# A fused chunk attention and multiplicative MLP kernel: another written order of steps, and pairs 6 and 7 on the path that joins partitions by DMA

## The chip, the cores and the metric

The kernel runs on one core of a Trainium2 chip. The core has five engines with a queue of instructions each: PE (matrix products, with a lane PEld for loading weights), DVE (vector work), ACT (scalar work and copies), POOL and SP. In this kernel POOL and SP do little but issue DMA transfers. Each engine works through its queue in order; semaphores make one engine wait for another. The metric is device time in microseconds (us), the median of several runs.

## The reference

Attention in chunks of 64 rows, without a mask and within each chunk alone, then a multiplicative MLP on the joined heads:

```
scores = scale * q_c @ k_c^T          # 8 batches, 8 heads, 9 chunks of 64 rows, head width 64
attn   = softmax(scores)              # over the 64 keys of the chunk
x      = (attn @ v_c), heads side by side   # 4608 tokens x 512
a, b   = x @ w1, x @ w2               # 512 -> 1024
out    = ((a * b) @ w3) @ w_out       # 1024 -> 1024 -> 512
```

All inputs and the output are float32. The kernel computes in bfloat16 with float32 sums, multiplies w3 by w_out once (the product w3o, 1024 x 512), and leaves out the maximum of the softmax, with a second path for inputs where that would not do.

## The kernel before

The 4608 tokens are cut into 18 pairs (p = 0 to 17) of 256 tokens, four chunks each, and two pairs make a group g. The whole program is one written list, ORDER, of short names that is walked once; every step issues its instructions at once, and each engine keeps the order of the list. So the list alone sets what stands behind what on PE, DVE, ACT, POOL and SP. A step name is a letter with its numbers:

- POOL issues the loads, with a cast to bfloat16: q, k, v of a pair (256 KB, 256 KB and two of 128 KB; some are cut in two), i (quarters of w1 and w2), o (w_out), h (w3). At most eight loads are under way: each waits for the one eight places ahead of it. q of pair p + 5 also waits until the transposes of pair p have left its buffer, v until the P step that last read its buffer. The steps x11 and x12 make POOL wait for N11.1 and N12.1.
- DVE: T p.s transposes q (s = 0) or k (s = 1) in 32 x 32 blocks (line 201). N p.u divides by the softmax sum (lines 261 and 264), X p.u transposes the result for the MLP (line 297 or 305), M p.j multiplies a and b (line 366), V transposes w3 (line 407).
- PE, all by the helper on line 95: S p are the scores, P p the product with v, A p.j and B p.j the products with w1 and w2 for one slice j, O p the output product for a pair, W the product of w3 and w_out, D fills the time at the start with zeros.
- ACT: E p is the exponential (line 234), C p.j copies a out of PSUM (line 351), Y p copies the output of a pair out of PSUM (line 396), Z copies w3o (line 420).
- SP issues Q p, the store of a pair, and G and H, moves between partitions inside the core (line 193).

Pairs 0 to 3 run A and B for one pair at a time (four slices of two times 256 columns), the later ones for a group (eight slices of 512 columns, named by the group's even pair: A4.0 to A4.7 belong to pairs 4 and 5).

There are two forms of the attention. The first leaves the head's 64 columns split over blocks of 32 partitions: S needs 64 small products that add up in twos, P 64. The second, for pairs 8 to 17, joins halves by DMA: G g.a (two steps of four moves, `qkT` to `qkm`, 128 KB each) ahead of S, which then takes 32 products of 64 x 64, as does P; X then writes `xm`, and H g.a (two steps of four moves, 64 KB each) brings it to `xt` ahead of A and B. The bound is `p < 8` in the code.

The buffers that couple the engines: four PSUM tiles of two banks for all of S, P (two tiles), A with B, O and W, given out in list order as they come free; three copies of a (`a_sb`); two of `e`; two of `qkT`, `qkm`, `xm` and `o_sb`; three of `xn` and `ab`; four of `xt`; five of `qk`; six of v, where pair p takes number p % 6. The first half of an A/B tile holds a, the second b; M reads the copy of a and, from PSUM, b.

In the old list each A p.j is followed on PE by B p.j, and C p.j stands behind both:

```
A4.2 E7 T10.0 B4.2 C4.2 T10.1 P7 v13
```

The functions that the diff touches, and what calls them:

Of the kernel before, what the change touches and what calls it, by code (L numbers as in the profile page):

```python
# [8 lines left out]
ORDER = """  # L9
R0 R1 v0 q1 k1 i0 v1 i1 i2 q2 k2 v2 i3 q3 k3 v3 q4 k4 v4 o h0 h1 D0.0.0.16.64 K0 T0.0 K1 T0.1 q5 k5  # L10
v5 S0 T1.0 E0 P0 D0.1.0.4.512 T1.1 q6 k6 v6 N0.0 S1 D1.0.0.5.512 X0.0 N0.1 X0.1 A0.0 E1 B0.0 C0.0 P1
M0.0 A0.1 N1.0 X1.0 B0.1 C0.1 N1.1 A0.2 X1.1 B0.2 C0.2 M0.1 A1.0 T2.0 B1.0 C1.0 M0.2 A1.1 T2.1 q7 k7
v7 B1.1 C1.1 M1.0 S2 M1.1 A0.3 E2 T3.0 B0.3 C0.3 P2 M0.3 A1.2 N2.0 X2.0 B1.2 C1.2 N2.1 A1.3 X2.1
B1.3 C1.3 M1.2 A2.0 T3.1 q8 k8 v8 B2.0 C2.0 M1.3 S3 T4.0 A2.1 E3 M2.0 B2.1 T4.1 q9 k9 C2.1 P3 v9
M2.1 A2.2 N3.0 B2.2 C2.2 X3.0 A2.3 N3.1 B2.3 X3.1 C2.3 M2.2 S4 M2.3 A3.0 E4 B3.0 C3.0 A3.1 M3.0 B3.1
C3.1 V0 A3.2 M3.1 B3.2 C3.2 V1 A3.3 M3.2 B3.3 C3.3 V2 W0 M3.3 V3 W1 Z0 V4 V5 W2 Z1 V6 V7 T5.0 Z2 W3
T5.1 q10 k10 T6.0 T6.1 P4 v10 q11 k11 Z3 S5 N4.0 O0 E5 X4.0 N4.1 X4.1 T7.0 O1 T7.1 Y0 Q0 T8.0 P5 v11
q12 k12 Y1 S6 T8.1 O2 Q1 E6 N5.0 X5.0 N5.1 X5.1 O3 T9.0 T9.1 Y2 G4.0 P6 v12 q13 k13 A4.0 N6.0 B4.0
G4.1 Y3 X6.0 N6.1 C4.0 A4.1 X6.1 B4.1 C4.1 M4.0 Q2 S7 Q3 M4.1 A4.2 E7 T10.0 B4.2 C4.2 T10.1 P7 v13
q14 k14 A4.3 M4.2 B4.3 N7.0 C4.3 A4.4 X7.0 M4.3 B4.4 C4.4 N7.1 A4.5 M4.4 B4.5 C4.5 X7.1 S8 M4.5 S9  # L20
E8 A4.6 T11.0 B4.6 E9 T11.1 P8 v14 q15 k15 C4.6 A4.7 M4.6 G5.0 B4.7 C4.7 N8.0 A6.0 M4.7 B6.0 N8.1
C6.0 G5.1 A6.1 X8.0 B6.1 M6.0 C6.1 X8.1 P9 v15 A6.2 M6.1 N9.0 B6.2 C6.2 N9.1 A6.3 M6.2 B6.3 C6.3
X9.0 A6.4 M6.3 B6.4 C6.4 X9.1 A6.5 T12.0 H4.0 B6.5 C6.5 M6.4 A6.6 M6.5 B6.6 T12.1 H4.1 C6.6 S10 S11
M6.6 E10 A6.7 T13.0 B6.7 E11 P10 T13.1 C6.7 O4 M6.7 G6.0 N10.0 N10.1 X10.0 G6.1 P11 Y4 X10.1 O5
N11.0 N11.1 x11 q16 k16 v16 Q4 X11.0 X11.1 T14.0 A8.0 H5.0 Y5 B8.0 T14.1 C8.0 A8.1 M8.0 B8.1 H5.1
C8.1 T15.0 A8.2 B8.2 M8.1 C8.2 T15.1 Q5 A8.3 B8.3 C8.3 M8.2 G7.0 S12 M8.3 S13 E12 A8.4 T16.0 B8.4
E13 G7.1 P12 T16.1 C8.4 A8.5 B8.5 M8.4 C8.5 N12.0 A8.6 M8.5 B8.6 C8.6 N12.1 x12 q17 k17 v17 A8.7
M8.6 B8.7 C8.7 X12.0 P13 M8.7 A10.0 X12.1 B10.0 C10.0 N13.0 A10.1 M10.0 B10.1 N13.1 C10.1 A10.2
X13.0 B10.2 M10.1 C10.2 X13.1 S14 S15 M10.2 E14 A10.3 H6.0 T17.0 B10.3 E15 P14 T17.1 C10.3 A10.4
H6.1 M10.3 B10.4 C10.4 N14.0 A10.5 M10.4 B10.5 G8.0 C10.5 N14.1 A10.6 M10.5 B10.6 C10.6 X14.0 P15  # L30
G8.1 X14.1 A10.7 M10.6 B10.7 N15.0 C10.7 O6 N15.1 M10.7 X15.0 X15.1 H7.0 S16 Y6 S17 O7 E16 E17 H7.1
P16 Y7 O8 Q6 N16.0 Q7 N16.1 X16.0 X16.1 P17 Y8 A12.0 N17.0 Q8 B12.0 N17.1 C12.0 A12.1 X17.0 B12.1
M12.0 C12.1 X17.1 A12.2 M12.1 H8.0 B12.2 C12.2 A12.3 M12.2 B12.3 C12.3 H8.1 A12.4 M12.3 B12.4 C12.4
A12.5 M12.4 B12.5 C12.5 A12.6 M12.5 B12.6 C12.6 A12.7 M12.6 B12.7 C12.7 O9 M12.7 O10 Y9 Q9 A14.0 Y10
B14.0 C14.0 Q10 A14.1 M14.0 B14.1 C14.1 A14.2 M14.1 B14.2 C14.2 A14.3 M14.2 B14.3 C14.3 A14.4 M14.3
B14.4 C14.4 A14.5 M14.4 B14.5 C14.5 A14.6 M14.5 B14.6 C14.6 A14.7 M14.6 B14.7 C14.7 O11 M14.7 O12
Y11 Q11 A16.0 Y12 B16.0 C16.0 Q12 A16.1 M16.0 B16.1 C16.1 A16.2 M16.1 B16.2 C16.2 A16.3 M16.2 B16.3
C16.3 A16.4 M16.3 B16.4 C16.4 A16.5 M16.4 B16.5 C16.5 A16.6 M16.5 B16.6 C16.6 A16.7 M16.6 B16.7
C16.7 O13 M16.7 O14 Y13 Q13 O15 Y14 Q14 O16 Y15 Q15 Y16 Q16 O17
"""  # L40


LOW, HIGH = 2.0 ** -60, 2.0 ** 60


@with_exitstack
def first_path(
# [12 lines left out]
    B, H, S, D = q.shape  # L60
# [3 lines left out]
    CH = 64  # L64
# [11 lines left out]
    W = D + 1  # L76
# [215 lines left out]

    def do_X(p, u):
        g, m = divmod(p, 2)
        if p < 8:
            t0 = m * PT + u * UT
            inorder(nc.vector.transpose(  # L297
                new_xt(g)[:].rearrange("p (o t) -> p o t", o=KO)[:, :, t0:t0 + UT]
                .rearrange("p o (m y) -> p m o y", y=BL),
                xn_t[p][:, u].rearrange("p r (c n) (z o) -> p (r c) o n z", c=2, o=KO)))  # L300
# [52 lines left out]
    def do_M(p, j):  # L353
        g = p // 2
        if g not in ab_t:
            ab_t[g] = msb.tile([P, FO, GT], bf, tag="ab", bufs=3, name="ab")
        if p < 4:
            o = ab_t[g][:, 2 * j:2 * j + 2, p % 2 * PT:(p % 2 + 1) * PT]
            view = lambda t: t.rearrange("p (j t) -> p j t", j=2)
        elif p < 8:  # L360
            o = ab_t[g][:, j]
            view = lambda t: t
        else:
            o = ab_t[g][:, j].rearrange("p (c s y) -> p s c y", s=2, y=BL)
            view = lambda t: t.rearrange("p (s c y) -> p s c y", s=2, y=BL)
        inorder(nc.vector.tensor_mul(o, view(a_t.pop((p, j))[:]), view(ps_t.pop((p, j))[:, 1, :])))  # L366
# [201 lines left out]
```

## Time and profile before

| | us |
|---|---|
| median of 3 runs | 244.77 (244.47 to 246.03) |
| span of the profiled execution | 242.9 |
| PE busy | 226.7 (93%) |
| DVE busy | 154.3 (64%) |
| ACT busy | 85.2 (35%) |
| POOL busy, issuing loads | 83.7 (34%) |
| granted clock of PE, mean | 1.00 |

The span runs from the first to the last instruction of one profiled execution, the page gives no other time of that execution; the median of the timed runs is 1.9 us above it. Busy time of PE is counted to modelled ends of pipelined matmuls, so the rows of a group may overlap a little. Digits in the page's slices are tenths, one digit for 6.1 us. A row of the timeline reads: start, length, engine and line, operation, output <- input, shape, count, and in brackets the idle time of that engine just ahead of it with what ended it. A row of the chain: start, length, what. A row of the waits: who waited, for whom, us in all, times, longest.

### The profile page before, as it was taken

How to read it: one execution, taken by the hardware profiler on the slowest of the kernel's cores; microseconds unless marked ns; L12 is line 12 of the kernel's file. 1: busy time of each engine (PE TensorE's matmuls, PEld its weight loads, DVE VectorE, ACT ScalarE, POOL GpSimd, SP SyncE). 2: the span in 40 equal slices, each digit the busy share in tenths (PEclk: the TensorE clock that was granted, in tenths of full speed). 3: DMA queues.
4: the chain of work that ended last, by engine and by line, in shares of the span. 5: the costliest groups of instructions: out<-in, count | busy, mean ns of one | idle time of the engine just before them, and what ended most of it. 6: DMA issues, size and time to landing. Idle time of an engine off the chain costs nothing.

```text
span 242.9 us, 6385 instructions
## 1 busy us (share of the span) xinstructions
PE 226.7 (93%) x2753; PEld 120.2 (49%) x2753; DVE 154.3 (64%) x235; ACT 85.2 (35%) x116; POOL 83.7 (34%) x114
## 2 busy tenths in 40 slices
PE   1189989999999999999999999999999999999994
PEld 1147868874445444444444444444444444444443
DVE  1756799699799588999998899918540332143000
ACT  2412423423333344425336234162332332322322
POOL 7856976656986345764160230000000000000000
PEclk9999999999999999999999999999999999999999
DMA  6999999999999999999999793735502200400244
GB/s 173 179 185 181 185 169 200 196 193 171 167 173 218 222 228 259 179 224 196 205 236 223 221 139 91 163 88 209 142 0 89 87 0 0 173 3 1 86 173 173
DMA packets 93597, 37.65 MB, mean 155 GB/s; under 512 B 75008, under 2 KB 86528, under 8 KB 93568
## 3 DMA queue, kind: packets, MB, share of 16 engines
q0 software_dynamic: 82592, 18.88, 83.9%
q1 hardware_dynamic: 9936, 17.83, 24.0%
q10 hardware_dynamic: 1040, 0.52, 0.8%
q8 instruction: 21, 0.34, 0.6%
q14 instruction: 8, 0.07, 0.1%
HBM read 38.80 MB, written 9.44 MB: 199 GB/s over the span
## 4 chain that ended last, share of the span: by engine, by line
PE 72%; DMA 16%; DVE 4%; SPq 3%; POOL 2%; issue 1%; ACT 0%; DVEq 0%; POOLq 0%
PE ab_ps L95 39%; PE o_ps L95 23%; PE w_ps L95 6%; DMA w<-in_moe_w_dram 4%; DMA qkm<-qkT 3%; SPq L193 3%; DMA qk<-in_q_dram 3%; DMA qk<-in_k_dram 3%; DMA xt<-xm 3%; PE pv L95 2%; PE s_ps L95 2%; DVE qkT L201 2%; POOL vbuf L98 1%; POOL w L98 1%; DVE xt L297 1%
## 5 line engine op out<-in xcount | busy, mean ns | idle before, releaser
L95 PE MATMUL ab_ps<-xt,w 128*128 128x512 bf16 (+1 forms) x688 | 127.4, 342 | 0.7 <-DVE xt L297 0.6
L95 PEld LDWEIGHTS <-w 128*128 128x128 bf16 x704 | 67.1, 98 | 56.1 <-issue 1.8
L366 DVE TENSOR_TENSOR ab<-a_sb,ab_ps 128x512 bf16<-128x512 f32 x71 | 47.8, 674 | 43.4 <-ACT a_sb L351 43.1
L351 ACT COPY a_sb<-ab_ps 128x512 f32<-128x512 f32 x71 | 41.6, 586 | 81.3 <-PE ab_ps L95 81.0
L95 PE MATMUL o_ps<-w3o,ab 128*128 128x512 bf16 (+1 forms) x296 | 63.9, 373 | 0.0
L201 DVE STREAM_TRANSPOSE qkT<-qk 128x1024 bf16<-128x1024 bf16 x36 | 45.1, 1291 | 7.2 <-ACT qk L144 5.5
L95 PEld LDWEIGHTS <-ab 128*128 128x128 bf16 x296 | 28.5, 98 | 32.2
L98 POOL DMA_DIRECT2D vbuf<-in_v_dram x40 | 33.9, 855 | 20.4 <-DMA qk<-in_q_dram 5.2
L396 ACT COPY o_sb<-o_ps 128x1024 f32<-128x1024 f32 x17 | 17.2, 1012 | 45.3 <-PE o_ps L95 41.3
L264 DVE TENSOR_TENSOR xn<-pv,rcs 128x512 bf16<-128x512 f32 x36 | 24.9, 692 | 1.4
L98 POOL DMA_DIRECT2D qk<-in_q_dram x23 | 18.1, 790 | 8.9 <-DMA qk<-in_k_dram 2.4
L98 POOL DMA_DIRECT2D qk<-in_k_dram x23 | 18.0, 783 | 6.5 <-DMA vbuf<-in_v_dram 3.7
L234 ACT ACTIVATE e<-s_ps 128x1024 bf16<-128x1024 f32 x16 | 15.9, 1026 | 1.7 <-PE s_ps L95 1.3
L95 PE MATMUL w_ps<-wo,w3T 128*128 128x512 bf16 x64 | 14.0, 379 | 0.0
L305 DVE STREAM_TRANSPOSE xm<-xn 128x512 bf16<-128x512 bf16 x20 | 13.5, 696 | 0.2
L261 DVE RECIPROCAL rcs<-pv 128x8 f32<-128x8 f32 x36 | 6.9, 193 | 10.4 <-PE pv L95 10.4
L98 POOL DMA_DIRECT2D w<-in_moe_w_dram x16 | 11.1, 695 | 5.3 <-DMA wo<-in_moe_w_out_dram 2.9
L95 PEld LDWEIGHTS <-e 64*32 64x32 bf16 (+1 forms) x832 | 7.8, 97 | 8.7 <-issue 6.9
L95 PE MATMUL pv<-vbuf,e 64*32 64x65 bf16 (+1 forms) x832 | 10.2, 197 | 1.8 <-ACT e L234 1.1
L297 DVE STREAM_TRANSPOSE xt<-xn 128x512 bf16<-128x512 bf16 x16 | 11.4, 711 | 0.5
L389 DVE COPY o_sb<-o_ps 128x256 f32<-128x256 f32 x1 | 0.4, 425 | 16.0 <-PE o_ps L95 16.0
L95 PEld LDWEIGHTS <-qkT 32*64 32x64 bf16 x512 | 5.5, 117 | 10.1 <-DVE qkT L201 7.9
(29 smaller groups left out, 54.2 us busy)
## 6 DMA issues: line engine op xcount, KB each, us to landing
out_dram<-o_sb SPq DMA_DIRECT2D x17, 512.0 KB, 3.3
qkm<-qkT SPq DMA_DIRECT2D x40, 128.0 KB, 4.0
vbuf<-in_v_dram POOLq DMA_DIRECT2D x32, 128.0 KB, 8.2
w<-in_moe_w_dram POOLq DMA_DIRECT2D x16, 256.0 KB, 9.9
qk<-in_q_dram POOLq DMA_DIRECT2D x11, 256.0 KB, 6.8
qk<-in_k_dram POOLq DMA_DIRECT2D x11, 256.0 KB, 7.8
xt<-xm SPq DMA_DIRECT2D x40, 64.0 KB, 3.2
wo<-in_moe_w_out_dram POOLq DMA_DIRECT2D x4, 256.0 KB, 7.1
```

The source lines that it names most:

```text
L95: return inorder(nc.tensor.matmul(*a, **kw))
L98: return inorder(nc.gpsimd.dma_start(dst, src))
L193: inorder(nc.sync.dma_start(dst, src))
L201: inorder(nc.vector.transpose(qkT_t[g][:, :, p % 2, s, heads(h)].rearrange("p e h (y t) -> p h t e y", t=2), qk_t[p][:, s, heads(h)].rearr ...
L234: inorder(nc.scalar.activation(e_t[p][:, :, heads(hh)], s_t[p][:].rearrange("p u (h q) -> p u h q", q=CH)[:, :, heads(hh)], Exp, scale=sca ...
L261: inorder(nc.vector.reciprocal(rc, pv[:, :, :, D:W]))
L264: inorder(nc.vector.tensor_mul(xn_t[p][:, u], pv[:, :, :, 0:D], rc.to_broadcast([P, 2, 4, D])))
L297: inorder(nc.vector.transpose(new_xt(g)[:].rearrange("p (o t) -> p o t", o=KO)[:, :, t0:t0 + UT] .rearrange("p o (m y) -> p m o y", y=BL), ...
L305: inorder(nc.vector.transpose(xm_t[g][:, u, :, m].rearrange("p o (c y) -> p c o y", y=BL), xn_t[p][:].rearrange("p u r m d -> p (u r) m d" ...
L351: inorder(nc.scalar.copy(a_t[p, j][:], ps_t[p, j][:, 0, :]))
L366: inorder(nc.vector.tensor_mul(o, view(a_t.pop((p, j))[:]), view(ps_t.pop((p, j))[:, 1, :])))
L396: inorder(nc.scalar.copy(o_sb[:], ps_t.pop(p)[:]))
```

## The change

Three things. First, the bound `p < 8` becomes `p < MOVED` with MOVED = 6, so pairs 6 and 7 (group 3) take the joined form: the list has the new steps G3.0, G3.1, H3.0 and H3.1. Second, the list is another one from behind B0.2 on; A and B of several slices are interleaved, and a C may stand ahead of its B; pairs come in another order in places (P9 ahead of P8, S13 ahead of S12, O1 ahead of O0, O2 behind O7). Third, v buffers are given out in the order in which P steps free them. Of the old list the diff below shows the first and last changed lines; the new one is whole.

```
--- before.py
+++ after.py
@@ -9,37 +9,38 @@
 ORDER = """
 R0 R1 v0 q1 k1 i0 v1 i1 i2 q2 k2 v2 i3 q3 k3 v3 q4 k4 v4 o h0 h1 D0.0.0.16.64 K0 T0.0 K1 T0.1 q5 k5
 v5 S0 T1.0 E0 P0 D0.1.0.4.512 T1.1 q6 k6 v6 N0.0 S1 D1.0.0.5.512 X0.0 N0.1 X0.1 A0.0 E1 B0.0 C0.0 P1
-M0.0 A0.1 N1.0 X1.0 B0.1 C0.1 N1.1 A0.2 X1.1 B0.2 C0.2 M0.1 A1.0 T2.0 B1.0 C1.0 M0.2 A1.1 T2.1 q7 k7
-v7 B1.1 C1.1 M1.0 S2 M1.1 A0.3 E2 T3.0 B0.3 C0.3 P2 M0.3 A1.2 N2.0 X2.0 B1.2 C1.2 N2.1 A1.3 X2.1
-B1.3 C1.3 M1.2 A2.0 T3.1 q8 k8 v8 B2.0 C2.0 M1.3 S3 T4.0 A2.1 E3 M2.0 B2.1 T4.1 q9 k9 C2.1 P3 v9
-M2.1 A2.2 N3.0 B2.2 C2.2 X3.0 A2.3 N3.1 B2.3 X3.1 C2.3 M2.2 S4 M2.3 A3.0 E4 B3.0 C3.0 A3.1 M3.0 B3.1
...
-C16.3 A16.4 M16.3 B16.4 C16.4 A16.5 M16.4 B16.5 C16.5 A16.6 M16.5 B16.6 C16.6 A16.7 M16.6 B16.7
-C16.7 O13 M16.7 O14 Y13 Q13 O15 Y14 Q14 O16 Y15 Q15 Y16 Q16 O17
+M0.0 A0.1 N1.0 X1.0 B0.1 C0.1 N1.1 A0.2 X1.1 B0.2 A1.2 A1.0 M0.1 C0.2 T2.0 T2.1 B1.2 M0.2 S2 C1.2 q7
+E2 M1.2 P2 B1.0 N2.0 k7 N2.1 A1.3 B1.3 X2.0 C1.0 X2.1 M1.0 T3.0 A2.0 C1.3 A2.3 T3.1 C2.0 A2.2 q9
+B2.0 B2.2 C2.2 M1.3 M2.0 S3 A2.1 T4.0 B2.3 T4.1 q8 B2.1 E3 C2.3 M2.2 P3 C2.1 M2.3 M2.1 S4 N3.0 E4
+N3.1 A1.1 A0.3 X3.0 P4 B0.3 X3.1 C0.3 B1.1 N4.0 M0.3 C1.1 N4.1 A3.0 A3.2 k8 A3.1 M1.1 X4.0 V3 C3.2
+B3.2 A3.3 B3.1 V2 M3.2 C3.1 v9 C3.3 B3.3 k9 V0 M3.1 W1 V1 M3.3 V4 W0 V5 Z0 T5.1 V6 T5.0 V7 X4.1 W2
+T6.0 T6.1 q10 T7.1 Z1 C3.0 S5 W3 E5 B3.0 Z2 Z3 v7 P5 T7.0 N5.0 N5.1 X5.1 O1 X5.0 A4.0 Y1 T8.0 T8.1
+q11 G3.0 B4.0 k11 O0 M3.0 G3.1 A4.7 T9.0 C4.0 Y0 M4.0 T9.1 B4.7 C4.7 S6 S7 M4.7 T10.0 E6 E7 A4.6
+C4.6 q12 P6 B4.6 N6.0 N6.1 M4.6 A4.2 X6.0 C4.2 A4.5 P7 B4.2 G4.0 N7.0 B4.5 A4.1 X6.1 C4.5 v8 N7.1
+A4.3 B4.3 k10 X7.0 G4.1 M4.5 M4.2 C4.3 v10 Q1 B4.1 C4.1 S8 X7.1 S9 M4.3 M4.1 E8 q14 H3.0 E9 O3 T11.1
+Y3 T11.0 P9 N9.0 N9.1 H3.1 q15 T10.1 A4.4 B4.4 C4.4 P8 A6.0 q13 C6.0 N8.0 M4.4 B6.0 A6.7 N8.1 G5.0
+M6.0 k12 A6.1 T12.0 A6.4 A6.2 X8.0 C6.1 B6.2 B6.7 C6.7 B6.1 C6.2 G5.1 B6.4 Q0 M6.7 O4 X9.0 v11 M6.1
+S10 C6.4 M6.4 k13 T14.0 X8.1 M6.2 X9.1 T12.1 E10 H4.0 A6.3 A6.6 Q3 C6.3 k15 Y4 B6.6 T13.0 C6.6 O5
+T13.1 B6.3 M6.6 A6.5 Y5 M6.3 P10 N10.0 C6.5 S11 B6.5 E11 k14 H4.1 A8.0 M6.5 P11 N10.1 C8.0 N11.0 v12
+B8.0 M8.0 T15.1 X10.0 N11.1 G6.0 A8.1 C8.1 T14.1 G6.1 Q4 A8.4 T15.0 O7 O2 X10.1 B8.1 Y7 Q5 S13 B8.4
+X11.0 C8.4 Y2 v13 X11.1 A8.2 E13 M8.1 M8.4 P13 S12 N13.0 B8.2 E12 C8.2 N13.1 H5.0 Q7 M8.2 q16 A8.7
+H5.1 k16 P12 N12.0 N12.1 B8.7 X12.0 O6 G7.0 A10.0 q17 B10.0 G7.1 C8.7 X13.1 T16.0 k17 Y6 X13.0 C10.0
+A10.2 T17.1 x11 A10.4 Q2 C10.4 M10.0 C10.2 T17.0 B10.2 T16.1 B10.4 A8.6 M8.7 M10.4 H6.0 C8.6 G8.0
+B8.6 M8.6 A8.3 S14 v14 S15 M10.2 C8.3 A8.5 E14 C8.5 B8.3 X12.1 A10.1 B8.5 G8.1 B10.1 M8.3 v16 C10.1
+M8.5 v17 E15 M10.1 H6.1 A10.7 C10.7 P14 N14.0 N14.1 X14.0 S16 B10.7 A10.3 E16 v15 A12.0 B10.3 Q6
+C10.3 C12.0 M10.3 O9 M10.7 B12.0 Y9 A12.4 C12.4 M12.0 P15 N15.0 S17 N15.1 B12.4 X15.0 X15.1 E17 O8
+P16 M12.4 X14.1 Y8 H7.0 N16.0 N16.1 A12.5 H7.1 P17 N17.0 B12.5 A12.2 N17.1 B12.2 C12.2 A14.7 A14.0
+C12.5 M12.5 A10.5 B14.0 C14.0 X16.0 C10.5 X17.0 B10.5 M12.2 Q9 M14.0 A12.3 M10.5 A12.6 B12.6 C12.6
+C14.7 M12.6 H8.0 A12.7 X17.1 B14.7 Q8 B12.3 A14.5 M14.7 C12.3 M12.3 A14.6 B12.7 C14.5 C12.7 A12.1
+C14.6 M12.7 B14.5 B14.6 A14.2 B12.1 M14.5 C12.1 A10.6 M14.6 A14.3 X16.1 B14.2 B14.3 M12.1 C14.2
+M14.2 B10.6 O13 C10.6 C14.3 M14.3 H8.1 Y13 A14.4 C14.4 M10.6 A14.1 A16.0 O12 B14.4 Y12 M14.4 B16.0
+C16.0 A16.5 C14.1 A16.1 B16.1 B16.5 M16.0 C16.1 B14.1 C16.5 M14.1 M16.1 A16.6 B16.6 A16.3 B16.3
+A16.4 C16.3 M16.5 B16.4 C16.4 Q13 C16.6 A16.7 M16.3 M16.6 A16.2 C16.7 O15 B16.2 x12 C16.2 Y15 B16.7
+Q15 O10 M16.7 Q12 O14 Y10 Q10 O11 Y14 Y11 M16.2 M16.4 Q14 O16 Y16 Q11 Q16 O17
 """
 
 
+MOVED = 6
 LOW, HIGH = 2.0 ** -60, 2.0 ** 60
 
 
@@ -162,10 +163,13 @@
 
         inorder(nc.gpsimd.tensor_copy(tick[:], xn_t[p][0:1, 1, 0, 0, 0:1]))
 
+    vb_t, vb_free = {}, list(vbuf)
+
     def load_v(p):
+        vb_t[p] = vb_free.pop(0)
         for u in range(2):
             for at, b, c, m in spans(4 * p + 2 * u, 2):
-                load(vbuf[p % 6][at * CH:(at + m) * CH, u, :, 0:D],
+                load(vb_t[p][at * CH:(at + m) * CH, u, :, 0:D],
                      v[b, :, c * CH:(c + m) * CH, :].rearrange("h p d -> p h d"))
 
     def load_w(dst, ap, n0, n1):
@@ -216,7 +220,7 @@
         if p not in s_t:
             s_t[p] = psum("s_ps")
         for h in range(H)[heads(hh)]:
-            if p < 8:
+            if p < MOVED:
                 for e in range(2):
                     for i in range(NB):
                         mm(s_t[p][half[i % 2], i // 2, h * CH:(h + 1) * CH],
@@ -239,21 +243,22 @@
 
 
         e = e_t[p]
+        vb_free.append(vb_t[p])
         for u in range(2):
             if (p, u) not in pv_t:
                 pv_t[p, u] = psum("pv")
             pv = pv_t[p, u]
             for m in range(4):
-                if p < 8:
+                if p < MOVED:
                     for g in range(NB) if hh is None else (2 * hh, 2 * hh + 1):
                         for r in range(2):
                             mm(pv[blk[g], r, m * W:(m + 1) * W],
                                lhsT=e[half[r], u, 2 * g + m % 2, m // 2 * BL:(m // 2 + 1) * BL],
-                               rhs=vbuf[p % 6][half[r], u, 2 * g + m % 2, 0:W], start=True, stop=True)
+                               rhs=vb_t[p][half[r], u, 2 * g + m % 2, 0:W], start=True, stop=True)
                 else:
                     for g, r in ((0, 0), (1, 1), (1, 0), (0, 1)):
                         mm(pv[half[g], r, m * W:(m + 1) * W], lhsT=e[half[r], u, 4 * g + m, :],
-                           rhs=vbuf[p % 6][half[r], u, 4 * g + m, 0:W], start=True, stop=True)
+                           rhs=vb_t[p][half[r], u, 4 * g + m, 0:W], start=True, stop=True)
 
     def do_N(p, u):
         pv = pv_t.pop((p, u))[:, :, 0:4 * W].rearrange("p r (m w) -> p r m w", w=W)
@@ -292,7 +297,7 @@
 
     def do_X(p, u):
         g, m = divmod(p, 2)
-        if p < 8:
+        if p < MOVED:
             t0 = m * PT + u * UT
             inorder(nc.vector.transpose(
                 new_xt(g)[:].rearrange("p (o t) -> p o t", o=KO)[:, :, t0:t0 + UT]
@@ -325,7 +330,7 @@
 
     def do_AB(p, j, f, which):
 
-        if p >= 8:
+        if p >= MOVED:
             rhs = new_xt(p // 2)[:].rearrange("p (s o t) -> p o s t", s=2, o=KO)
         else:
             rhs = new_xt(p // 2)[:].rearrange("p (o t) -> p o t", o=KO)
@@ -357,7 +362,7 @@
         if p < 4:
             o = ab_t[g][:, 2 * j:2 * j + 2, p % 2 * PT:(p % 2 + 1) * PT]
             view = lambda t: t.rearrange("p (j t) -> p j t", j=2)
-        elif p < 8:
+        elif p < MOVED:
             o = ab_t[g][:, j]
             view = lambda t: t
         else:
```

More of the change, by code (lines that the diff above doesn't have):

```diff
@@ L16 @@
[L16 to L37, printed above, removed]
```

## The prediction

> **What bounds the kernel now.** I read the page's busy shares first, then the waits, then the chain that ended last, then the timeline of TensorE.
>
> ```profile
> PE 226.7 (93%) x2753; PEld 120.2 (49%) x2753; DVE 154.3 (64%) x235; ACT 85.2 (35%) x116; POOL 83.7 (34%) x114
> PE   1189989999999999999999999999999999999994
> DVE  1756799699799588999998899918540332143000
> ```
>
> TensorE (PE) is busy 226.7 of 242.9 us, and from the fifth slice on its digit is 9. What it still waits for is in the list of waits of PE:
>
> ```profile
> PE z_ps L95 <- DVE qkT L201: 7.4, 1, 7.4
> PE pv L95 <- ACT e L234: 1.1, 1, 1.1
> PE ab_ps L95 <- DVE xt L297: 0.6, 2, 0.3
> ```
>
> The 7.4 us end at 9.8 us, in the part of the order that stays. Behind that, apart from two gaps of 0.3 us ahead of A1.0 and A2.0 and some short ones with no releaser (0.7 us in P2, 0.5 us in S7), PE waits for nothing. The windows say the same: from 31.8 to 168 us it is busy 135.3 of 136.2 us. So this kernel is bound by the sum of PE's work, and a new order can lower its time only by what PE has less to do; every wait that the order puts on PE is paid in full. Why there are none: in the old list every A is followed by its own B, then the copy C, and between a score step S and its P stand other matmuls. One place has nothing there, S0 E0 P0, and shows the bare price:
>
> ```profile
> 12.02 0.75 PE L95 MATMUL pv<-vbuf,e 64*32 64x65 bf16 x64 [1.13 <-ACT e L234]
> ```
>
> That is one exponential (1.03 us at 10.94) and 0.1 us of hand-over, all seen by PE.
>
> **What the change saves.** The prices of the attention steps are in the chain:
>
> ```profile
> 65.93 0.63 PE pv L95 x64
> 66.56 0.64 PE s_ps L95 x64
> ...
> 95.77 0.64 PE s_ps L95 x64
> 96.41 1.83 PE ab_ps L95 x8
> 98.25 0.38 PE pv L95 x32
> ```
>
> An unjoined P is 64 matmuls in 0.63 us, an unjoined S 64 in 0.64 us. At 95.77 the 64 matmuls are S8 and S9 together, so a joined S takes 0.32 us; a joined P takes 0.38 us. Pairs 6 and 7 save 2 x (0.32 + 0.25) = 1.1 us of PE. The 0.3 us ahead of A2.0 go too, since more matmuls stand there: 1.4 us in all. The transposes X keep their cost (696 ns joined, 711 ns not). The joined path adds 8 qkm and 8 xt moves on SP's queue, 5.0 to 6.0 us of issue per eight. That queue idles 135.8 us waiting for output copies; G3 stands ahead of G4 and 10 us of PE work ahead of S6. I cost the issue at nothing; uncovered it would be 6 us each.
>
> **What the change adds.** In the new list, 27 B steps stand behind their own C (none before), and in the built program the first matmul of such a B then waits for that copy: they share a PSUM tile. The trace of before has no such wait. Bounds: nothing, if the copy is done when PE gets there, and 1.13 us, the nearest row, if all is bare; I take the copy's own row, 0.59 us plus the 0.02 to 0.05 us between engines that the chain shows, and subtract the PE work between. A half step (A or B) is 5.29/6 = 0.88 us, E 1.03 us, Y 1.01 us, M 0.6 us in a row, a transpose T 1.21 us in a row. Walking the new list, the places where the cover is too short:
>
> 1. B1.2 S2 P2: nothing between S2 and P2 on PE, so E2 is bare, 1.1 us as at P0. Before it, M0.1 and two T's (3.0 us after X1.1) against three half steps (2.8): 0.2. Together **1.3**.
> 2. B3.1 B3.3: ACT's list is C3.1, C3.3, and C3.1 waits for B3.1. Two copies bare: **1.25**.
> 3. S6 S7 A4.6 P6 B4.6: ACT does E6, E7 (1.95), then C4.6 (0.6); with hand-over 2.65, less A4.6 and P6 (1.25): **1.4**.
> 4. A6.0 C6.0 B6.0 and A8.6 C8.6 B8.6, with nothing between: 0.65 each, **1.3**.
> 5. B8.4 A8.2 P13: ACT does C8.4, Y2, E13 (0.6 + 1.0 + 1.0 + 0.1), less A8.2 (0.88): **1.8**.
> 6. A10.2 A10.4 B10.2: ACT does C10.4 first, then C10.2: **1.25**.
> 7. Small ones: P14 behind C10.1 and M10.1 (0.45), B8.0 (0.25), B10.7 (0.2): **0.9**.
> 8. A14.7 needs H7.1, which needs X14.1. Behind P15 DVE does two N, two X, M12.4, X14.1 (4.3 us), then SP issues four moves (0.75 each) and the last lands 3.2 us after its issue: some 9.9 us; PE has 8.95 us of work from P15 to A14.7: **1.0**. H3.1 to A6.0 in the same way: **0.2**.
>
> Sum 10.4 us; less 1.4: **+9.0 us**. None is given back later: PE has no wait behind them that could shrink, and the last 60 us of the new list are covered (between C and B lie two steps or more, and O15, O10, O14, O11, O16, O17 follow at 3.46 us each against 1.01 us for the copy and 3.3 us for a store).
>
> Loads: v7 now stands behind q10, which waits for T5.0 (some 62 us); issued by 67 us and landing 8.2 us later (the row of vbuf), P7 at some 86 us has 11 us to spare. q13 waits for T11.0 (some 95 us) with k12, v11, k13 queued behind it on POOL; the first needed of them, k12, is asked for by T12.1 some 17 us later. DVE's own queue waits behind T12.1 and PE behind DVE, so this cover matters; without it the lateness is paid in full. The v buffers given out as they come free change only which P a load waits for. I cost all of this at nothing.
>
> Against its own execution the span becomes 242.9 + 9.0 = 251.9 us. The median of the runs, 244.77 us, lies 1.9 us above that span; with the same around it: **253.8 us**. A difference under 1% (2.4 us) is about what cannot be told from no change.
>
> **The rivals.**
>
> *The waits are half hidden* (chance 0.17). For: my walk counts from modelled ends, and DVE is at 90% from 67 to 130 us (56.5 of 63), so a PE held back lets DVE and the moves catch up; items 1 (0.2), 7 and 8 may vanish (2.1), and each bare copy may show half. Against: the P0 row. Price: about 4.5 us instead of 9, 249.3 us.
>
> *Late transfers* (chance 0.15). A move of qkm lands 4.0 us after its issue in the median but up to 9.2 us; xt 3.2 and up to 8.2. G3 before S6, H3 before A6.0 and H7 before A14.7 have no slack by my walk. Each that lands at its worst costs 5 us: one gives 258.8 us, two 263.8. For: loads keep the DMA at 9 tenths until 110 us. Against: in before all of these were hidden. [...]
>
> *Not slower* (chance 0.08). Mechanism: the single C step. If ACT, busy only 35%, reads each half tile so early that the copy ends within the PE work already queued, no B waits, and S2 to P2 falls where PE would have waited for v2 or w1 loads anyway. Then only the 1.4 us saved remain, and perhaps the 0.02 us by which a half step in the crowded stage (0.88) exceeds one in the last stage (13.81/16 = 0.863), some 1 us over 56 of them: 242.3 us. It decides once six of my nine items show under 0.2 us. That the joining does nothing for pairs 6 and 7 would only add 1.1 us to any case.
>
> **How the numbers follow.** Forecast, waits of 7 to 12 us net: 0.60. The range 248.5 to 260 holds the forecast, most of the half-hidden case and one late move; it leaves out two late moves and the not-slower case. Faster by over 1%: 0.05, within 1%: 0.05, slower: 0.90.
>
> **What would show it.** PE's list of waits should hold some 4 us for ACT e and about 5 us for ACT a_sb, a kind that is absent now, with P2 and P13 the longest single ones; PE's busy time should fall by about 1 us; POOL and the loads should show no new wait of PE. It is wrong if PE waits for DVE or for moves more than for ACT, if the a_sb waits are missing, or if the last chain runs through loads.

## The result, and the profile after

| | before | after |
|---|---|---|
| median of the runs, us | 244.87 (244.47 to 246.03, 4 runs) | 263.38 (262.88 to 264.36, 4 runs) |
| span of the profiled execution, us | 242.9 | 261.9 |

The ratio is 1.077, with a 95% interval from 1.073 to 1.081: slower by 18.5 us between the medians. The forecast was slower by 9.0 us, and its range ended at 260. The direction was right; half of the loss was not foreseen.

The page of the changed kernel: the busy shares, the slices of PE and DVE, the granted clock of PE, and the row of the instruction queue q8.

```profile
PE 230.1 (88%) x2625; PEld 120.8 (46%) x2625; DVE 154.0 (59%) x235; ACT 83.3 (32%) x116; POOL 83.9 (32%) x114
...
PE   1389597779999899899899797999989999998994
...
DVE  1839669697979688838785686456754530332000
...
PEclk9999989999999999999999999999999999999999
...
q8 instruction: 20, 0.33, 0.5%
```

PE has 128 products fewer and is busy 3.4 us longer. That is no contradiction: the busy time is counted to modelled ends, so a matmul in front of a stop counts with its whole length (0.19 us for the product of S4 ahead of its stop, where 64 in a row take 0.71 us), and one at a low clock with more (0.42 us for a product of 128x256 instead of 0.27). The row of slices shows the loss better: at 6.5 us a digit, a 5 and three 7s between 26 and 59 us, two more 7s between 144 and 164, and 8s strewn over the rest. One digit of the clock, behind the 5, is 8 instead of 9. The instruction queue q8 brings 20 packets instead of 21; that row will matter. A move of `qkm` lands 6.7 us after its issue in the median, against 4.0 before.

PE's list of waits in the changed kernel (who waited, for whom, us in all, times, longest):

```profile
PE ab_ps L96 <- ACT a_sb L356: 6.3, 8, 1.2
PE pv L96 <- ACT e L238: 3.9, 3, 1.7
PE s_ps L96 <- issue: 1.9, 1, 1.9
PE pv L96 <- issue: 1.6, 1, 1.6
...
PE ab_ps L96 <- issue: 1.1, 1, 1.1
PE ab_ps L96 <- DVE rcs L266: 1.0, 1, 1.0
PE o_ps L96 <- ACT o_sb L401: 0.7, 1, 0.7
PE ab_ps L96 <- DVE both L286: 0.6, 1, 0.6
```

The first two rows are the forecast: 6.3 us for copies of a (about 5 foretold, a kind that was absent; 1.5 us of the 6.3 stand ahead of B10.5 and B14.7, which were not foretold), and 3.9 us for exponentials (some 4 foretold, one of them P0's as before). The rest was not foreseen. "issue" means that PE waited for nothing that the profile shows.

To place every loss I took, from the timeline of PE, the time from each step's first matmul to the next step's, and subtracted the usual price of the step (a half step 0.92 us in the first pairs and 0.864 later, and the prices of the prediction for S, P and O). What is over comes to 7.4 us before and 27.7 us after. The difference, 20.3 us, less 1.1 us of saved matmuls and 0.2 us of earlier start, is the 19.0 us by which the span grew:

| where | forecast, us | found, us |
|---|---|---|
| the eight numbered places of the prediction | 10.4 | 10.5 |
| copies ahead of B10.5 and B14.7, counted as covered | 0 | 1.8 |
| gaps of PE for "issue" in P2, S4, A3.0, less those of before in P2 and S7 | 0 | 3.7 |
| B1.0, A1.3, B1.3 at a lower clock | 0 | 1.5 |
| DVE or a move late: A8.0 1.1, S6 0.6, S10 0.4, S16 0.4 and less; E for A6.6 0.3 | 0 | 3.1 |
| the last 60 us: O10 0.9, O15 0.3 | 0 | 1.2 |
| start, small waits of before that are gone, and the remainder | -0.3 | -1.7 |
| joined steps of pairs 6 and 7 | -1.1 | -1.1 |
| sum | 9.0 | 19.0 |

Three of the unforeseen losses stand in one stretch of PE's timeline of the changed kernel:

```profile
27.02 0.71 PE L96 MATMUL s_ps<-qkT 32*64 32x64 bf16 x64 [0.17 <-DVE qkT L205]
28.87 0.66 PE L96 MATMUL pv<-vbuf,e 64*32 64x65 bf16 x61 [1.14 <-ACT e L238]
31.12 0.21 PE L96 MATMUL pv<-vbuf,e 64*32 64x65 bf16 x3 [1.59 <-issue]
31.26 5.01 PE L96 MATMUL ab_ps<-xt,w 128*128 128x256 bf16 x29
...
44.01 0.50 PE L96 MATMUL s_ps<-qkT 32*64 32x64 bf16 x37
46.45 0.41 PE L96 MATMUL s_ps<-qkT 32*64 32x64 bf16 x27 [1.95 <-issue]
```

The exponential between S2 and P2 is bare, as foretold. But P2 stops again before its last three products, for 1.6 us, and S4 stops in its middle for 2 us, at no boundary of the written list. And the 29 products behind P2 take 5.01 us, where 0.115 us each would be 3.3.

### The profile page after: what moved, and what is told of

Same layout as the page of the kernel before. It is cut to its first block, busy times and chain, and to the rows that moved or that the text cites. A ratio compares the mean times of both kernels' runs of the same rounds, so it can differ in the third digit from the quotient of the medians.

```text
span 261.9 us, 6172 instructions
## 1 busy us (share of the span) xinstructions
PE 230.1 (88%) x2625; PEld 120.8 (46%) x2625; DVE 154.0 (59%) x235; ACT 83.3 (32%) x116; POOL 83.9 (32%) x114
## 4 chain that ended last, share of the span: by engine, by line
PE 71%; DVE 9%; ACT 6%; issue 6%; DMA 5%; SPq 2%; DVEq 0%; ACTq 0%
PE ab_ps L96 41%; PE o_ps L96 21%; DVE qkT L205 4%; ACT a_sb L356 3%; DMA qkm<-qkT 3%; PE s_ps L96 3%; PE z_ps L96 3%; PE pv L96 2%; DMA raw<-in_q_dram 2%; ACT e L238 2%; DVE xn L269 2%; SPq L197 2%; PE w_ps L96 1%; DVE ab L371 1%; DVE w3T L412 1%
## 5 line engine op out<-in xcount | busy, mean ns | idle before, releaser
L96 PE MATMUL ab_ps<-xt,w 128*128 128x512 bf16 (+1 forms) x688 | 131.5, 345 | 9.7 <-ACT a_sb L356 6.3
L96 PEld LDWEIGHTS <-w 128*128 128x128 bf16 x704 | 68.0, 99 | 67.2 <-issue 11.3
L356 ACT COPY a_sb<-ab_ps 128x512 f32<-128x512 f32 x71 | 40.5, 588 | 95.8 <-PE ab_ps L96 95.7
L310 DVE STREAM_TRANSPOSE xm<-xn 128x512 bf16<-128x512 bf16 x24 | 16.1, 687 | 0.1
L99 POOL DMA_DIRECT2D w<-in_moe_w_dram x16 | 11.1, 696 | 4.5 <-DMA vbuf<-in_v_dram 1.4
L412 DVE STREAM_TRANSPOSE w3T<-w 128x1024 bf16<-128x1024 bf16 x8 | 9.7, 1219 | 1.4 <-PE w_ps L96 1.4
```

Of the source, the lines that this page charges most:

```text
L96: return inorder(nc.tensor.matmul(*a, **kw))
L99: return inorder(nc.gpsimd.dma_start(dst, src))
L310: inorder(nc.vector.transpose(xm_t[g][:, u, :, m].rearrange("p o (c y) -> p c o y", y=BL), xn_t[p][:].rearrange("p u r m d -> p (u r) m d" ...
L356: inorder(nc.scalar.copy(a_t[p, j][:], ps_t[p, j][:, 0, :]))
L412: inorder(nc.vector.transpose(w3T_t[f][:].rearrange("p k (f y) -> p f k y", y=BL), w3[:, NB * f:NB * (f + 1), :].rearrange("p f (k x) -> p ...
```

## The experiments

Where a run has one execution, its span is compared with the 261.9 us of the changed kernel, called the new list here. Four executions of that had spans from 261.3 to 262.8 us, so a difference under 1.5 us in the whole span says little, and the steps are read instead. Of each diff only the steps that move are shown.

**1. All copies behind their B.**

```
-A4.6 C4.6 q12 P6 B4.6
+A4.6 q12 P6 B4.6 C4.6
...
```

All 27 such C move in this manner.

> The changed kernel (span 261.9 us) with one thing undone: each of the 27 copies C that stand ahead of their own B is moved to right behind it. Theory 1, the waits of B for C are paid in full: the eight gaps in which PE waited for a copy of a (B3.3 1.28, B4.6 1.09, B6.0 0.83, B8.0 0.37, B10.2 1.32, B8.6 0.84, B10.5 1.32, B14.7 0.46; 7.5 us) are gone, span 254 to 255.5 us. Rival: they stand for lateness that shows elsewhere once they are gone (DVE, moves between partitions, buffers); span above 258.5 us, with new waits of PE for DVE.

Span 258.6 us, time 260.15 us. The eight waits for `a_sb` are gone from PE's list, and only 3.3 us with them. Two rows of this run's list show what took their place:

```profile
PE s_ps L96 <- DVE ab L371: 1.4, 1, 1.4
PE pv L96 <- DMA qk<-in_q_dram: 1.3, 1, 1.3
```

S13 now waits 1.4 us behind B8.1 for a PSUM tile that DVE has to free. P5 waits 1.3 us in its middle; the row names a load, but ACT's copy Z2, which stands behind C3.0 now, ends at 75.08 us, and PE goes on at 75.13. S10 loses 1.1 us instead of 0.4, part of it to a late `qkm` move. The rival was nearer: the waits taken from PE were in part handed on, to DVE, to ACT's queue and to a move. Of the 7.5 us that the theory expected, 4.2 were given back.

**2. A half step between S2 and P2, and 3. four idle products there.**

```
-S2 C1.2 q7 E2 M1.2 P2 B1.0
+S2 C1.2 q7 E2 M1.2 B1.0 P2
```

```
-S2 C1.2 q7 E2 M1.2 P2 B1.0
+S2 C1.2 q7 E2 M1.2 D2.2.0.4.512 P2 B1.0
```

> The changed kernel with B1.0 moved to stand between S2 and P2. Theory 2, three costs hang on that place: the wait for E2 falls from 1.14 to about 0.2 us, the gap inside P2 (1.79 us behind matmul 478, which by this theory is a fetch of instructions and not a wait for data) falls to about 0.9, and with PE less idle between 27 and 31 us the clock stays at 1.00 between 31.2 and 35.5 us instead of 0.60, worth 1.5 us. Span 258 to 259 us. Rival: only the wait for E2 goes, the clock falls all the same: span 260.8 us.

> The new list with one step more: four matmuls with zeros (512 columns each, some 0.9 us) between S2 and P2, where TensorE waits 1.2 us for E2. They compute nothing that is used and hide no wait. Theory (the clock gate answers to how little TensorE has done in the microseconds around S2 and P2): the granted clock stays at 1.00 after P2, B1.0, A1.3 and B1.3 keep their price, and the span is some 1.5 us below the 261.9 of the new list: 260.2 to 260.7. Rival (the slow steps behind P2 come from something else, such as data that arrive late): B1.0, A1.3 and B1.3 still take 1.5 us too long and the span is 261.7 to 262.5.

Spans 259.2 and 260.3 us. In (2) the wait for E2 shrinks to 0.16 us, but P2's gap for "issue" stays: 1.87 us from matmul to matmul, where about 0.9 was expected. The half step only takes the place of the wait for E2, so PE reaches the stop hardly later than before, at 29.5 us instead of 29.3. Counted from B0.2, A1.3 starts 0.9 us earlier than in the new list, clock apart. Most of the rest of the 2.7 us, 1.5, is the clock, which does not fall here: it is 1.00 from 31.2 to 35.5 us, where the new list has 0.60. (3) keeps the wait for E2 and fills it with products of zeros that nothing uses, and that alone gives 1.6 us. The windows of the new list and of (3), with columns length, PE busy (matmuls), granted clock, DMA share, GB/s:

```profile
27.00:31.20 4.20, 1.44 (x128) 1.00 1.84 181
31.20:35.50 4.30, 4.30 (x27) 0.60 2.01 173
```

```profile
27.00:31.20 4.20, 2.50 (x133) 1.00 1.82 181
31.20:35.50 4.30, 4.30 (x46) 1.00 2.01 173
```

After 4.2 us with 1.44 us of work the granted clock is 0.60 in the mean of the next 4.3 us, which 27 products fill; with 2.50 us of work it is 1.00 and 46 fit. Of the six profiled executions with this place as it is in the new list, five lost the clock there (the new list, runs 1, 6, 7 and 9; not run 4); of the three with a half step or the products of zeros in it (runs 2, 3 and 10), none. In the new list PE lost its clock behind a stretch in which it was not wholly idle: 1.44 of 4.2 us at work, with waits of 1.14 and 1.59 us.

**4. S4 away from P3, in the new list, and 5. S4 put right behind P3, in the old one.**

```
-P3 C2.1 M2.3 M2.1 S4 N3.0 E4 N3.1 A1.1
+P3 C2.1 M2.3 M2.1 N3.0 N3.1 A1.1 S4 E4
```

```
-P3 v9 M2.1 A2.2 N3.0 B2.2 C2.2 X3.0 A2.3 N3.1 B2.3 X3.1 C2.3 M2.2 S4 M2.3 A3.0 E4 B3.0
+P3 S4 E4 v9 M2.1 A2.2 N3.0 B2.2 C2.2 X3.0 A2.3 N3.1 B2.3 X3.1 C2.3 M2.2 M2.3 A3.0 B3.0
```

> The changed kernel with A1.1 between P3 and S4 (S4 and E4 moved behind A1.1). PE stood 2.14 us inside S4, behind matmul 734, with no releaser shown. Theory 3, a fetch of instructions that small matmuls outrun: the gap stays behind matmul 734, now inside S4 at its 29th product, and is shorter by about the 0.9 us that A1.1 takes: 1.2 us; span 261 us. Rival: a wait for data of S4; it stays at the 37th product or moves to the first one with its whole 2.1 us, or goes altogether.

> The kernel before (span 242.9 us, no gap at S4) with S4 and E4 moved to right behind P3. Theory 3: 128 small products stand together around matmul 734, which is now the 37th of S4, and a gap of 1 to 2.1 us opens there; span 244 to 245 us. Rival, the gaps come from the time or from the loads and not from the order: no gap behind matmul 734, span 242.5 to 243.3 us.

The reason to try this: counted in PE's order, the gaps for "issue" stand behind matmul 223, 478 and 1372 in the old list and behind 223, 478, 734 and 861 in the new one. The distances are 255 and 894 in the old list and 255, 256 and 127 in the new one, multiples of about 128, and the instruction queue brought 21 packets for 2753 matmuls and 20 for 2625, 131 matmuls a packet in the mean. My reading, inferred from these numbers alone, which these runs test: a packet brings the instructions of some 128 matmuls, and PE stops where it has used one up before the next has come. The two traces also have the time of each packet of that queue, and these agree: in the new list packets have landed at 29.70, 45.11 and 51.29 us, and the gaps in P2, S4 and A3.0 end at 31.12, 46.45 and 52.74; in the old list packets have landed at 30.05 and 86.12 us, and the gaps in P2 and S7 end at 31.53 and 87.72. Each gap ends 1.3 to 1.6 us after a landing.

In (4) the gap at S4 shrinks from 2.14 to 1.17 us from matmul to matmul and stands at S4's 29th product instead of its 37th, eight earlier because A1.1's eight now stand ahead: the number 734 stays. A3.0's gap, at 861, grows from 1.4 to 1.7. The span is 259.8 us, where 261 was expected; the clock did not fall this time, though P2's waits were the same, which is 1.5 us of the difference. In (5) the old list gets the gap of the new one:

```profile
41.85 0.50 PE L95 MATMUL s_ps<-qkT 32*64 32x64 bf16 x37 [0.30 <-DVE qkT L201]
44.75 0.41 PE L95 MATMUL s_ps<-qkT 32*64 32x64 bf16 x27 [2.40 <-issue]
```

It is longer than expected, 2.6 us from matmul to matmul, and the clock is 0.69 in the mean from 44.2 to 48.4 us, 1.00 in the 4.2 us before: span 247.7 us, 4.8 more than before, for one score step and its exponential moved. Run (3) shows the same from another side: its four products of zeros shift S4's gap by four, from the 37th to the 33rd product. To the end of the gap, the gap included, it is 5.9 us from behind matmul 606 in S4, 6.3 from behind 734 in A3.0, 5.3 from behind 1244 in S7, and 4.8 and 4.9 from behind 350 in P2 of the new and of the old list. By my reading so little work within about 128 matmuls makes the gap: 64 small products of S or P are 0.6 us, the eight of a half step in the first pairs 0.9. It does not decide alone: in run 8 below, whose list is the old one up to P2, P2 has no gap.

**6. T14.0 later on DVE.**

```
-C6.4 M6.4 k13 T14.0 X8.1
+C6.4 M6.4 k13 X8.1
...
+N10.1 T14.0 C8.0
```

> The new list with one transpose of q and k, T14.0, moved from ahead of X8.1 to behind N10.1 in VectorE's order, so that VectorE does not stand 2.4 us at it while the qkm buffer is still being read or filled. Theory: the wait of A8.0 for N10.0 (1.1 us in the new list) shrinks to under 0.3 us, and the span falls by about 1 us, to 260.7 to 261.2. Rival (VectorE is late in this stretch whatever it does first): A8.0 or the step behind it waits as before, and the span stays within 0.3 us of 261.9.

Span 260.7 us, as expected. In the new list T14.0 holds DVE for 2.4 us until a `qkm` move has landed, and A8.0 then waits 1.1 us. DVE's timeline of the new list has the row:

```profile
118.90 1.33 DVE L205 STREAM_TRANSPOSE qkT<-qk 128x1024 bf16<-128x1024 bf16 x1 [2.37 <-DMA qkm<-qkT]
```

Here that wait is gone. But A8.1 now waits 0.45 us more and S10 0.4: of 1.5 us won at A8.0 and A6.6, 0.9 is lost again between S10 and A8.4. The other 0.6 us of the span are at S6 and A14.7.

**7. Pairs 6 and 7 not joined, in the new list, and 8. joined, in the old list.**

```
-MOVED = 6
+MOVED = 8
...
-q11 G3.0 B4.0 k11 O0 M3.0 G3.1 A4.7
+q11 B4.0 k11 O0 M3.0 A4.7
...
-q14 H3.0 E9 O3 T11.1
+q14 E9 O3 T11.1
...
-N9.1 H3.1 q15
+N9.1 q15
```

```
-T7.1 Y0 Q0 T8.0 P5
+T7.1 Y0 Q0 G3.0 G3.1 T8.0 P5
...
-Y1 S6 T8.1 O2 Q1 E6 N5.0
+Y1 T8.1 O2 Q1 q13 k13 N5.0
...
+C4.2 S6 M4.1 S7 E6 A4.3 M4.2 B4.3 E7 C4.3 P6
...
+X7.0 S8 X7.1 S9 H3.0 H3.1 E8 M4.6 A4.7
...
+O3 M4.7 T11.0 T11.1 Y3 Q3 G5.0 O4 N8.0 N8.1 Y4 Q4 A6.0
```

In the second, the bound `p < 8` of the old kernel becomes 6.

> The new list with pairs 6 and 7 as before (not joined: no G3, no H3, the limit 8 instead of 6). Theory: joining saved 1.1 us of matmuls and cost some 0.6 us at S6 and 0.3 us at A6.0, so the span without it is 261.9 + 0.3, between 261.7 and 262.7. Rival (the eight qkm and eight xt moves that joining adds hold up SP's queue and the later moves, G5 and T14.0 among them): without them the wait of A8.0 goes as well and the span falls by 1 to 2 us, to 260 to 261.

> The old list with only one part of the change: pairs 6 and 7 join the groups whose q, k, x change partitions by DMA (G3 behind T7.1, S6 and S7 together, H3 behind X7.1, and O4 with its copy and store ahead of A6.0 as cover for the moves), every B ahead of its C as before. Theory (the joining saves 1.1 us of matmuls at no cost if the moves have cover, and the short gap in S7 that fetching its instructions makes goes too): the span falls to 241.2 to 242.2 and the time by 1.0 to 1.8 us, to 0.993 to 0.996 of before. Rival (the moves on SP's queue come late for S6 or for A6.0, or hold up later stores and moves): the time is the same or longer.

(7): span 263.4 us. The clock stayed low for longer in this execution (0.50 in the mean from 31.2 to 35.5 us, where the new list has 0.60; 2.6 us lost behind P2 instead of 1.5); without that it is 0.5 us over the new list. So in the new list the joining would gain about half of the 1.1 us of matmuls that it saves; with one execution of this run that is not shown.

(8): 252.32 us against 244.83, ratio 1.031 (1.029 to 1.034). I had expected a gain. The profiled execution is the fastest of five, with a span of 249.0 us and a granted clock of 1.000; the others had 250.4 to 251.4 us at 0.985 to 0.993, so the clock has a share in the 7.5 us. PE's list of waits:

```profile
PE ab_ps L95 <- DMA xt<-xm: 2.7, 1, 2.7
PE ab_ps L95 <- DVE xt L297: 1.6, 2, 1.2
PE s_ps L95 <- DMA qkm<-qkT: 1.5, 1, 1.5
```

and the chain that ended last, in the same stretch:

```profile
71.10 1.02 ACT o_sb L396
72.14 6.62 DMA out_dram<-o_sb
78.78 6.76 DMA qkm<-qkT
85.58 0.91 PE s_ps L95 x63
...
101.53 5.72 DMA xt<-xm
107.71 3.61 PE ab_ps L95 x16
```

G3's moves stand behind the store Q0 on SP, which waits for ACT's copy until 72.1 us. From then to S6's second product it is 13.4 us: 6.7 for eight moves one after the other, 6.8 until the last lands. H3 is the same: X7.1 is done at 96.3 us, A6.0 starts at 107.7. Some 10 us of other work, the cover that the prediction counted for S6, would not reach, nor does the step O4 moved ahead of A6.0. The waits hold DVE up too, and 2.2 us follow at P11 and O5.

**9. v buffers by number, in the new list.**

```
-vb_t[p] = vb_free.pop(0)
+vb_t[p] = vbuf[p % 6]
```

> The new list with the v buffers given out by number (pair modulo 6) as before, instead of as they come free. Theory (no step of TensorE waits for v in either form): the span is within 0.5 us of the 261.9 of the new list, apart from the stretch behind P2, where the clock makes some 0.5 us of difference between executions. Rival (a v buffer that comes free late holds up POOL's queue with k11, k12, q13 behind it): a wait for v, or for qkT through the loads, appears and the span is over 263.5.

Span 264.5 us: over the 263.5 that the rival named, but without the wait for v, or for `qkT` through the loads, that was to show it. Counted by steps, the 2.6 us are 1.0 more behind P2 (the clock was 0.87 from 27.0 to 31.2 us and 0.50 from 31.2 to 35.5, against 1.00 and 0.60), 1.1 at S6, which waited 1.7 us for its `qkm` move instead of 0.6, and 0.3 at the start. S6's wait was between nothing and 0.6 us in the other runs of the new list. The eight moves took 6.9 us to issue here instead of 5.1, and the last landed 7.7 us after its issue instead of 7.8, so it is the issue that was late. One execution cannot tell whether the loads, asked for in other places by this edit, held it up, or whether it varies by itself. What the third part of the change is worth stays open, within some 1 us.

**10. All the repairs in one list.**

```
-E2 M1.2 P2 B1.0
+E2 M1.2 B1.0 P2
...
-S13 B8.4 X11.0 C8.4 Y2 v13 X11.1 A8.2 E13
+S13 E13 B8.4 X11.0 C8.4 Y2 v13 X11.1 A8.2
...
-A10.4 Q2 C10.4 M10.0 C10.2 T17.0 B10.2 T16.1 B10.4
+A10.4 Q2 M10.0 T17.0 B10.2 C10.2 T16.1 B10.4 C10.4
...
-x12 C16.2 Y15
+x12 Y15 C16.2
```

Besides, S4 and T14.0 stand as in runs 4 and 6, C4.6, C6.0, C8.0, C8.6, C10.5 and C14.7 behind their B, and C3.1 behind B3.3.

> The new list with the steps moved that the two traces blame, and nothing else: B1.0 between S2 and P2; S4 and E4 behind A1.1; each of C3.1, C4.6, C6.0, C8.0, C8.6, C10.2, C10.5, C14.7 (and C10.4) behind its own B; E13 ahead of C8.4; T14.0 behind N10.1; C16.2 behind Y15. Theory (each wait is paid singly and goes singly): 7.5 us of waits for copies, 1.2 for E2, 1.8 for E13, 1.1 for A8.0, 0.9 at O10, some 0.6 of instruction fetch and 1.5 of low clock go, 14.6 us in all, and the span comes to 247 to 249 us. Rival (as when all copies were moved, waits that go come back in other places as PE gets ahead of DVE, ACT and the loads): less than 10 us go, and the span is above 252 us.

Time 253.92 us, 1.038 of before (1.033 to 1.043). The profiled execution is the fastest of four, with a span of 250.8 us and a granted clock of 1.000; the others had 252.0 to 252.3 us at 0.993, the clock of the new list, so some of them may have lost it still. Of 14.6 us 11.1 went in the profiled execution, and 9.5 between the medians: less than the theory expected, near the rival. From B10.7 to O17 the gain is 2.8 us, and the waits removed there (B10.5, B14.7, O10 and part of A14.7) sum to 2.85: paid singly, as in the prediction, where DVE is at 7 tenths or less. Up to there it is 8.3 of 11.9 us. What is left:

```profile
PE pv L96 <- issue: 1.9, 1, 1.9
PE pv L96 <- ACT e L238: 1.5, 3, 1.1
...
PE ab_ps L96 <- issue: 1.4, 1, 1.4
PE s_ps L96 <- issue: 1.1, 2, 1.0
```

Three gaps for "issue", at the same numbers 478, 734 and 861, are about half of the 8 us that still lie between the spans of this list and the old one; the rest are a dozen waits for DVE and moves of under 0.9 us each.

**11 and 12. The old list without its own gaps.**

```
-S7 Q3 M4.1 A4.2 E7 T10.0 B4.2 C4.2 T10.1 P7
+Q3 M4.1 A4.2 T10.0 B4.2 C4.2 S7 T10.1 M4.2 A4.3 E7 B4.3 C4.3 P7
```

The second has this too, and besides:

```
-A0.3 E2 T3.0 B0.3 C0.3 P2 M0.3 A1.2 N2.0 X2.0 B1.2 C1.2 N2.1 A1.3 X2.1
+A0.3 E2 T3.0 B0.3 A1.2 C0.3 P2 N2.0 X2.0 B1.2 C1.2 N2.1 A1.3 X2.1 M0.3
```

> The old list, nothing joined, with one score step moved: S7 from ahead of A4.2 to behind B4.2 (E7, P7 and N7.0 follow by one half step each, so that E7 and N7 keep their cover). Between matmuls 1244 and 1372, where a new packet of instructions has been needed, PE then has 6.2 us of work instead of 4.6. Theory (instruction fetch: a packet of 128 matmuls takes some 5.3 us to come, and the gap is what the work before it falls short by): the gap of 0.68 us in S7 goes and none comes elsewhere; the span falls by 0.5 to 0.7 us, to 242.2 to 242.4, the time to 0.997 to 0.998 of before. Rival (the gap belongs to S7 and the load of the DMA there, not to the matmul's number): it stays at S7, 0.5 us or more, and the time does not change.

> As the run before it in this call, and in the same manner at the other gap of the old list: A1.2 goes ahead of P2, so that there are 5.0 us of work instead of 4.2 from matmul 350 to 478, and M0.3 goes behind X2.1 on VectorE, which brings N2 and X2, that A2.0 waits for, 0.6 us forward. Theory (instruction fetch): the gap of 0.87 us in P2 shrinks to 0.3 or less, A2.0 waits no longer than now (0.4), and the span falls by another 0.5 to 1.0 us: 241.3 to 241.9, the time 0.993 to 0.996 of before. Rival: A1.2, no longer behind P2, leaves A2.0 waiting for X2.1 by 0.9 us more, and what the gap gives back is lost there: no difference between this and the run before it.

Both gaps are closed, as the expectations said: S7 runs through in (11), 64 products in 0.71 us, and in (12) PE's list has no wait of P2 for "issue". And neither is faster: 1.0011 of before (1.0001 to 1.0020) and 1.0011 (0.9998 to 1.0023). PE's timeline of (11):

```profile
88.70 0.71 PE L95 MATMUL s_ps<-qkT 32*64 32x64 bf16 x64
...
92.58 0.59 PE L95 MATMUL ab_ps<-xt,w 128*128 128x512 bf16 x2 [0.71 <-DVE ab L366]
```

The 0.7 us comes back four steps on, as a wait for DVE, and so it does in (12). But here DVE was held up by the edit itself: T10.0 writes the buffer that S7 reads, and now waits for the S7 that was moved back. DVE's timeline of (11):

```profile
89.48 2.50 DVE L201 STREAM_TRANSPOSE qkT<-qk 128x1024 bf16<-128x1024 bf16 x2 [1.09 <-PE s_ps L95]
```

So what S7's gap costs stays open. That P2's gap costs nothing is shown. In (12) A1.3 and S3 wait 0.4 and 0.5 us for DVE in its place. And in four executions that gap was 0.87 us (the old list), 0.57 (run 11) and none (runs 8 and 12), while S3 started 6.9 us after the start of T3.0 in each; T3.0 had waited 1.3 to 1.9 us for its load of q. There DVE, behind a load, is the bound, and PE's gap falls into time in which it would wait anyway.

## Why the prediction was wrong

The step that failed is not the pricing of the waits but what the sum left out: "None is given back later ... and the last 60 us of the new list are covered", and the costs put at nothing. The eight places came to 10.5 us, where 10.4 were forecast. Beside them the runs show 3.7 us of stops for "issue", 3.0 us in the part called covered, 1.5 us of low clock, and 3.1 us of DVE and moves: 11.3 us, of which 1.4 came back at the start and in small waits that were gone.

*What bounds the kernel.* "This kernel is bound by the sum of PE's work ... every wait that the order puts on PE is paid in full" is half right. Put on, a wait is paid: the eight numbered places came to 10.5 us against 10.4. But a wait taken away is not returned in full where DVE, or what DVE waits for, is nearly as late (runs 1, 6 and 10, and P2's gap in the old list). Behind PE's 93% stood a second bound, close enough to take back a gain of 1 us.

*The numbered places.* Found against forecast: 1 1.5 (1.3); 2 1.3 (1.25); 3 1.1 (1.4); 4 1.7 (1.3); 5 1.8 (1.8); 6 1.3 (1.25); 7 0.8 (0.9); 8 1.0 (1.2). The way of pricing, the copy's or exponential's own row less the work of PE between, holds. At A14.7 the row names DVE's `both`, the test of the softmax sums behind N17.1, but that was done at 189.33 us. The last move of H7.1 landed at 189.66 and PE went on at 189.86. So the later of the two was H7.1, which the prediction named.

*"The last 60 us of the new list are covered"* failed. In the list C10.5 stands behind C14.0 on ACT, so B10.5 waits 1.3 us behind B14.0; B14.7 waits 0.5, O15 0.3, and O10 0.9 for a tile that Y15 frees behind C16.2. I had checked B only right behind its own C and not walked ACT's queue: 3.0 us.

*Instructions cost nothing* was assumed without a word: the prediction named the 0.7 us in P2 and 0.5 us in S7 as "short ones with no releaser" and went on. They were the row to follow, and with them the row `PE z_ps <- issue` of 1.1 us, which the prediction does not name. Nor is PE's digit 9 from the fifth slice on, as it says: the sixth, with P2's gap in it, is 8. The new list sets S2 by P2 and P3 by S4, so from matmul 606 to 734 PE has 3.8 us of its own to do, where the old list takes 6.4. In all 3.7 us were lost.

*The clock* stands nowhere in the sum. In the new list the wait for E2 (1.14 us) and the gap in P2 (1.59 us) stand 0.7 us apart, PE works 1.44 of 4.2 us, and then the granted clock is 0.50 from 31.77 to 35.18 us: 1.5 us. With the columns as above:

```profile
28.36:31.77 3.41, 1.31 (x69) 1.00 2.00 173
31.77:35.18 3.41, 3.41 (x18) 0.50 1.95 178
```

Run 4 had the same waits (1.15 and 1.59 us) and kept its clock:

```profile
27.00:31.20 4.20, 1.47 (x126) 1.00 1.81 182
31.20:35.50 4.30, 4.12 (x40) 1.00 2.02 173
```

So whether these waits cost the clock differs between executions, and the runs do not show by what. Nor do they give a limit: the clock fell in or behind stretches of 4.2 us with 1.44 to 2.05 us of work (the new list, runs 1, 5, 6, 7 and 9), and stayed at 1.00 in run 4 with 1.47, and in run 8 in and behind 3.4 us with 0.67 us of work, ahead of A6.0.

*The moves cost nothing* failed in size here and altogether elsewhere. S6 lost 0.6 us, and A8.0 1.1 behind T14.0, which waited for a `qkm` move that the prediction did not follow through DVE's queue. Run 8 shows the price without cover: 13.4 us from the first issue to S6.

*The rivals.* "Not slower" and "half hidden" are refuted by the eight places. "Late transfers" had the right size of 258.8 to 263.8 us by luck: its three places, S6, A6.0 and A14.7, lost 1.6 us together, 1.2 of it forecast in item 8, and not 5 us each.

## What to carry to other kernels

A gap without a releaser is worth its own test: move the work around it and see whether it stays at the same matmul number. Here it stayed at 734 when eight matmuls were put ahead of it (run 4), and went from S7 when S7 stood behind other work (run 11); I read such gaps as instructions that came late. Look at short waits that stand close together as one: here two waits of 1.1 to 1.6 us within 4.2 us came with a lower clock in five of six executions. A row that names who ended a wait is to be checked against the times: twice the engine named was not the one. And ask of every wait what stands right behind it: adding the eight cost their full price here, taking waits away paid only up to the next engine that was nearly as late.

## What the runs showed of the hardware

- The instruction queue q8 brought 21 packets in the old list, with 2753 matmuls, and 20 in the new one, with 2625. PE's gaps for "issue" behind the first 20 us stood behind matmul 478 and 1372 in the old list and behind 478, 734 and 861 in the new one, and each ended 1.3 to 1.6 us after a packet of q8 had landed. From one matmul to the next they took 0.7 to 2.1 us there, and 2.6 us in S4 of run 5. That PE waited for the packet is inferred.
- The granted clock of the new list was 0.50 for 3.41 us, from 31.77 to 35.18 us, behind 3.41 us in which PE was at work 1.31 us; a matmul of 128 x 256 then took 0.21 us instead of 0.11 from start to start. In runs 7 and 9 the clock was 0.50 in the mean from 31.2 to 35.5 us; in run 4, with 1.47 us of work from 27.0 to 31.2 us, it was 1.00.
- Eight moves between partitions of 128 KB took 6.7 us to issue behind one another in run 8 and another 6.8 us until the last had landed, with loads under way; in the new list the issue took 5.1 us.
